# Product of attention, row sums, routing steps and zero rows given other places in the instruction order of a fused attention, MoE and expert kernel

## Chip, cores and metric

One core of a Trainium2 chip. The metric is the device time of one execution in microseconds (us): the median of three timed runs of the kernel before was 1121.9 us (1115.05 to 1123.45).

## What is computed

Three layers in a row on 2304 tokens of width 512. Attention: 32 pairs of batch and head of 576 queries, where of every row of scores only the 32 largest are kept:

```python
scores = scale * np.matmul(q, k.transpose(0, 1, 3, 2))
kth = np.partition(scores, -32, axis=-1)[..., -32:-31]
scores = np.where(scores >= kth, scores, -1e9)
attn = exp(scores - max) / (sum + 1e-9)
x = np.matmul(attn, v)
```

Then a dense layer `softplus(x @ w_in) @ w_out` with 2048 hidden units, and last eight experts: `expert = argmax(x @ w_gate)`, and each token gets `gate * (relu(x @ w1[expert]) @ w2[expert])` from the one expert that it was routed to.

## The kernel before

Five engines run their own instruction streams in order and wait for one another by semaphores. A scheduler at build time sets each stream: blocks of code carry a priority (`tc.high_priority`), and inside `tc.issue_after(x)` the instructions of the block that run on the engine of `x` are put behind `x` in that engine's order. This is an order alone; no semaphore comes with it.

**Part one** is one loop over 72 groups of attention, each of two tiles of 128 rows by 576 scores. Iteration i does the following.

- The scores of group i+1 (`emit_scores`, L372 on TensorE, copied by ScalarE at L380). Their PSUM buffer `ps_s` is a single one, so these matmuls wait until VectorE has read the scores of group i for the last time (L424).
- The search for the 32 largest of group i on VectorE (`emit_softmax`): rows are folded (L408 to L424), then four searches for 8 maxima (L414, L432) with three replacements (L428) between them, so three search rounds j = 0, 1, 2; then the mask (L440, or L443 with L444 on GpSimd). ScalarE takes the exponentials (L421), halves of the result are formed (L448 to L450), and a transposing DMA brings them into `pT` (L452, issued on SyncE's queue SP).
- The product with v of group j = i - 3 (`emit_av`, LAG = 3): matmuls L467 and L469 into the PSUM tile `m`, the row sums that come with it are inverted on VectorE (`rc`, L491 and L493), and ScalarE scales the result with them (L495). In before the product is ordered behind the last matmul of the scores that this very iteration issued, those of group i+1.
- Steps of the dense layer (`some_work`, 1.7 per iteration): units of one or two tiles of tokens, numbered 1 to 10, 16 steps each. A step is `layer1` (12 matmuls L554, softplus on ScalarE, its sum L563 on GpSimd) and, two steps later, `layer2` (L588 with f32 operands, one for each tile; from unit 9 on L585). These are called *dense steps* below.
- After each such step one step of a side queue, which holds generators. `route` (L612 to L663) is one for each finished tile: transposes, gate matmul, VectorE work on the logits, an exponential on ScalarE (L635) whose sum VectorE takes up (`gs`, L636), matmuls for the rank of each token in its expert, and DMAs that write the token's row to `rows` and its place to `table`. In before it is cut by `yield` into five steps. `clear_late` (L664 to L671), queued once unit 1 is done (`ZFILL = 1`), clears an `xr` buffer of the pool `x2p` on GpSimd (L667) and writes 1154 KB of zeros from it with two DMAs (L669) over the rows of tokens that come late. `early_slots` (L673 to L706), queued after unit 7, plans the first five slots of experts: the counts (matmul L676), and then five rounds on VectorE, each giving one pair of values in `early` (L704, L705).

**Part two** runs the slots: SyncE loads the pair of a slot into registers (L824, L825), reads 256 token numbers (`idx`, L829), loads the weights (L833, L836), GpSimd gathers the rows (`xg`, L841), TensorE transposes them (L863) and does the two matrix products (L893, L906). The first slots of part two are scheduled while the last dense steps still run.

The time falls into the attention with dense steps (to 777 us), the last dense steps (777 to 870 us) and the expert slots (870 us to the end).

Of the kernel before, what the change touches and what calls it, by code (L numbers as in the profile page):

```python
# [24 lines left out]
KD = DM // 128  # L25
# [33 lines left out]
C = 512  # L59
LAG = 3  # L60
SCALE = 1
ZFILL = 1
LATE = ((2, 8), (3, 0))
GLAG = 2
XAHEAD = 2
# [104 lines left out]
def part_one(tc, ctx, q, k, v, w_in, w_out, const, ident, before, ones, iota_e, reg_e, wg, ids,  # L170
# [182 lines left out]
        pair[m] = (q1, q2, kt, v16, sc)  # L353

    sc_t, pt_t, o_t, x_t = {}, {}, {}, {}
    tops, last_qk = [None], [None]

    def emit_qk(m, kind, ps, base):
        q1, q2, kt, v16, sc = pair[m]
# [25 lines left out]
    def emit_softmax(gi):  # L385
# [39 lines left out]
        for j in range(3):  # L425
            for i in n:
                to = wk[i] if flags is None else src[i]
                nc.vector.match_replace(out=to, in_to_replace=mx[:, i, 8 * j:8 * j + 8], in_values=src[i],  # L428
                                        imm_value=NEG)
                src[i] = to if flags is None else w2[:, i, :wide[j + 1]]  # L430
            for i in n:
                nc.vector.max(out=mx[:, i, 8 * j + 8:8 * j + 16], in_=src[i])  # L432
        if flags is not None and gi % FLB == FLB - 1:
            g0 = 2 * (gi - FLB + 1)
            nc.vector.tensor_tensor(out=flags[:, g0:g0 + 2 * FLB],
# [105 lines left out]
    def layer1(u):  # L541
# [9 lines left out]
        m = 0  # L551
        for c in range(KD):
            for p, r in ((0, 0), (0, 1), (1, 0)):
                nc.tensor.matmul(hps[:, :n], lhsT=w_in_s[:, c, j, p, o:o + 128], rhs=xT[:, 0:len(u.tiles), r, c, :],  # L554
                                 start=m == 0, stop=m == 3 * KD - 1)
                m += 1
        a = ep.tile([128, 256], F32, name="sa")
        nc.scalar.activation(a[:, :n], hps[:, :n], AF.Abs, scale=down)
# [18 lines left out]
    def layer2(u, f):  # L577
        if f == 0:
            u.y = [ps_y.tile([128, DM], F32, name="y") for _ in u.tiles]
        g = u.g.pop(f)  # L580
        for i in range(len(u.tiles)):
            cs = slice(i * 128, i * 128 + 128)
            if u.number >= TAIL:
                for m, (a, b) in enumerate(PASSES):
                    nc.tensor.matmul(u.y[i], lhsT=g[0][:, a, cs], rhs=g[1][:, b, :], start=f == 0 and m == 0,  # L585
                                     stop=f == KF - 1 and m == 2)
            else:
                nc.tensor.matmul(u.y[i], lhsT=g[:, cs], rhs=w_out_s[:, f, :], start=f == 0, stop=f == KF - 1)  # L588
        if f == KF - 1:
            for i, (key, spans) in enumerate(u.tiles):  # L590
                xr = x2p.tile([128, ROWW], F32, name="xr")
                nc.scalar.activation(xr[:, :DM], u.y[i], AF.Copy, scale=2.0 ** -8)
                side.append(route(xr, spans, ids_col(key), u.number > NU))
            if u.number == ZFILL:
                side.append(clear_late())
            if u.number == NU:
                side.append(early_slots())

# [13 lines left out]
    def route(xr, spans, col, after):  # L612
# [7 lines left out]
        lp = ps_h.tile([128, 512], F32, name="h")  # L620
        for c in range(KD):
            nc.tensor.matmul(lp[:, 0:E], lhsT=x2T[:, c, :], rhs=wg[:, c, :], start=c == 0, stop=c == KD - 1)
        lg = sm.tile([128, E], F32, name="lg")
        nc.vector.tensor_copy(lg, lp[:, 0:E])
        m8 = sm.tile([128, E], F32, name="m8")
# [3 lines left out]
        nm = sm.tile([128, 2], F32, name="nm")  # L629
        nc.vector.tensor_scalar(nm[:, 0:1], m8[:, 0:1], -1.0, None, op0=ALU.mult)  # L630
        nc.vector.tensor_copy(nm[:, 1:2], ix[:, 0:1])
        yield
        ex = sm.tile([128, E], F32, name="ex")
        gs = sm.tile([128, 1], F32, name="gs")
        nc.scalar.activation(ex, lg, AF.Exp, bias=nm[:, 0:1], accum_out=gs)  # L635
        nc.vector.tensor_scalar(gs, gs, 1e-9, None, op0=ALU.add)  # L636
        nc.vector.reciprocal(xr[:, DM:DM + 1], gs)
        oh = sm.tile([128, E], F32, name="oh")
        nc.vector.tensor_scalar(oh, iota_e, nm[:, 1:2], None, op0=ALU.is_equal)
        yield  # L640
        pp = ps_h.tile([128, 512], F32, name="h")
        nc.tensor.matmul(pp[:, 0:E], lhsT=before, rhs=oh, start=True, stop=False)
        nc.tensor.matmul(pp[:, 0:E], lhsT=ones, rhs=ohcum, start=False, stop=True)
        ds = sm.tile([128, E], F32, name="ds")
        nc.vector.tensor_tensor(out=ds, in0=pp[:, 0:E], in1=reg_e, op=ALU.add)
        nc.vector.tensor_tensor(out=ohcum, in0=ohcum, in1=oh, op=ALU.add)
# [17 lines left out]
    def clear_late():  # L664

        z = x2p.tile([128, ROWW], F32, name="xr")
        nc.gpsimd.memset(z, 0.0)  # L667
        for b, r0 in LATE:
            nc.sync.dma_start(rows[b * S:b * S + S, :].rearrange("(p r) a -> p r a", r=R)[:, r0:],  # L669
                              z[0:64].rearrange("p (o a) -> p o a", o=1).to_broadcast([64, R - r0, ROWW]))  # L670
        yield  # L671

    def early_slots():  # L673

# [68 lines left out]
    for i in range(-1, n + LAG):  # L743
# [15 lines left out]
        if to_scale and to_scale[0][1] <= i:  # L759
            with tc.high_priority(offset=AHEAD):  # L760
                prep_scale(to_scale.pop()[0])
        if i == -1:
            decode_some(2)
        if i + 1 < n:
            with tc.high_priority(offset=A_SC):
                emit_scores(i + 1)
        if 0 <= i < n:
            with tc.high_priority(offset=AHEAD):
                emit_softmax(i)
# [1 line left out]
                decode_some(DECR)  # L771
        j = i - LAG
        if j >= 0:
            with tc.high_priority(offset=A_AV), ExitStack() as behind_scores:
                if i + 1 < n:

                    behind_scores.enter_context(tc.issue_after(last_qk[0].ins))
                for x in groups[j]:
                    emit_av(*x)
            for u in units.get(j, []):  # L780
# [273 lines left out]
```

## Time and profile before

| | us |
|---|---|
| median of three timed runs | 1121.9 |
| lowest, highest | 1115.05, 1123.45 |
| the profiled execution | 1126.11 |
| its span in the trace | 1124.4 |

The profile is one execution. Its span is 1.7 us shorter than its time, and its time is 4.2 us above the median of the timed runs. Mean granted TensorE clock: 0.936. In the rows below PE is TensorE's matmuls, PEld its weight loads, DVE is VectorE, ACT ScalarE, POOL GpSimd, SP SyncE; SPq and POOLq are the DMA queues that these two issue on. A number in brackets behind a row is the time that the engine was idle ahead of it, with what ended that. Names without numbers are the program's tiles.

### The profile page before, as it was taken

To read this page: it belongs to the slowest core of one execution; us is meant where nothing else is said; L and a number is where in the kernel's file an instruction comes from. 1 tells how busy PE (TensorE), PEld (TensorE's weight loads), DVE (VectorE), ACT (ScalarE), POOL (GpSimd) and SP (SyncE) were. 2 spreads that over 40 slices of the span, in tenths; PEclk is the share of its full clock that TensorE was granted. 3 is DMA by queue.
4 is the path that set the end of the run, shared out by engine and by line. 5 is a ranking of instruction groups with operands and counts; after the bars stand their busy time and mean duration, and the time that the engine had idled before them with its cause. 6 is when DMAs were issued, how large, how long until landed. Compare 5 with 4: busy or idle time off the path is not lost.

```text
span 1124.4 us, 22653 instructions
## 1 busy us (share of the span) xinstructions
PE 895.9 (80%) x7146; PEld 646.0 (57%) x7146; DVE 948.4 (84%) x2980; ACT 798.7 (71%) x1898; POOL 638.0 (57%) x731
## 2 busy tenths in 40 slices
PE   1133257766887887899989999999999999999992
PEld 0012144433554564666556666566778889999981
DVE  4999999999968787999989899999556887767771
ACT  5767678886657777877888787877689655555560
POOL 3888889887466666766777666757423112111110
PEclk9996578997988898999999999999999999999996
DMA  8897788885467789635766664444601566666550
GB/s 191 193 197 157 175 179 168 182 193 108 71 110 110 135 137 137 126 74 96 145 131 125 104 106 74 83 74 82 201 19 24 119 234 223 250 206 246 201 189 18
DMA packets 295881, 157.18 MB, mean 140 GB/s; under 512 B 257524, under 2 KB 257652, under 8 KB 295732
## 3 DMA queue, kind: packets, MB, share of 16 engines
q1 hardware_dynamic: 292116, 145.73, 60.1%
q0 software_dynamic: 3616, 9.72, 2.5%
q8 instruction: 62, 1.02, 0.4%
q14 instruction: 87, 0.71, 0.3%
HBM read 77.89 MB, written 11.11 MB: 79 GB/s over the span
## 4 chain that ended last, share of the span: by engine, by line
PE 34%; DVE 28%; DMA 13%; issue 8%; POOL 7%; ACT 6%; SPq 2%; POOLq 0%; ACTq 0%; DVEq 0%
PE h L893 8%; PE y L906 8%; DVE mx L432 6%; PE h L554 5%; DVE wk L428 5%; PE y L588 4%; DMA pT<-p 4%; DVE xr L216 3%; DVE mk L443 2%; PE y L585 2%; POOL p L450 2%; DVE e L440 2%; DVE wk L424 2%; DMA w<-in_moe_w_in_dram 1%; POOL g L563 1%
## 5 line engine op out<-in xcount | busy, mean ns | idle before, releaser
L588 PE MATMUL y<-w_out_s,g 128*128 128x512 f32 x480 | 244.2, 634 | 31.3 <-POOL g L563 31.0
L554 PE MATMUL h<-xT,w_in_s 128*128 128x256 f16 (+1 forms) x1920 | 226.6, 268 | 23.4 <-DMA xT<-xh 10.1
L554 PEld LDWEIGHTS <-w_in_s 128*128 128x128 f16 x1920 | 173.6, 101 | 95.3 <-issue 60.3
L372 PE MATMUL s<-kt,q 128*128 128x512 f16 (+7 forms) x640 | 97.8, 315 | 131.5 <-DVE wk L424 87.7
L432 DVE MAX8 mx<-wk 128x8 f32<-128x144 f32 (+2 forms) x432 | 199.6, 494 | 0.2
L563 POOL TENSOR_TENSOR g<-g,sa 128x256 f32<-128x256 f32 (+1 forms) x160 | 118.7, 745 | 101.7 <-ACT sa L562 93.6
L450 POOL TENSOR_TENSOR p<-e,p 128x512 f16<-128x512 f32 x144 | 169.2, 1175 | 0.0
L448 ACT ACTIVATE p<-e 128x576 f16<-128x576 f32 x144 | 98.2, 684 | 73.6 <-DMA pT<-p 35.2
L372 PEld LDWEIGHTS <-q 128*128 128x128 f16 (+1 forms) x640 | 44.6, 107 | 174.9 <-DVE wk L424 70.9
L588 PEld LDWEIGHTS y<-w_out_s,g 128*128 128x128 f32 x480 | 86.5, 201 | 101.8 <-issue 61.3
L428 DVE MATCH_REPLACE8 wk<-mx,wk 128x144 f32<-128x144 f32 (+1 forms) x432 | 144.5, 340 | 0.1
L444 POOL TENSOR_TENSOR e<-e,mk 128x576 f32<-128x576 f32 x84 | 109.6, 1307 | 47.7 <-DVE mk L443 25.9
L873 POOL DMA_INDIRECT out_dram<-ot,idx x19 | 19.9, 1045 | 177.5 <-DVE ot L872 174.8
L893 PEld LDWEIGHTS h<-xT,wf 128*128 128x128 f32 x864 | 111.9, 191 | 5.3 <-ACT wf L854 0.2
L893 PE MATMUL h<-xT,wf 128*128 128x256 f32 x864 | 114.0, 283 | 0.0
L906 PE MATMUL y<-wf,hT 128*128 128x512 f32 x432 | 112.7, 399 | 0.0
L421 ACT ACTIVATE e<-s,bias 128x576 f32<-128x576 f32 x144 | 105.8, 770 | 2.1 <-POOL p L450 0.9
L467 PE MATMUL m<-v,pT 128*128 128x65 f16 (+1 forms) x1440 | 92.3, 200 | 9.7 <-ACT x L495 8.4
L467 PEld LDWEIGHTS <-pT 128*128 128x128 f16 (+1 forms) x1440 | 85.5, 105 | 16.3 <-issue 12.5
L906 PEld LDWEIGHTS y<-wf,hT 128*128 128x128 f32 x432 | 76.8, 189 | 13.2
L380 ACT ACTIVATE s<-s 128x1152 f32<-128x1152 f32 x72 | 80.5, 1119 | 4.8 <-PE s L372 4.7
L469 PE MATMUL m<-v,pT 128*128 128x64 f16 (+1 forms) x800 | 75.7, 200 | 0.0
(193 smaller groups left out, 1900.2 us busy)
## 6 DMA issues: line engine op xcount, KB each, us to landing
w1r<-in_moe_w_dram SPq DMA_DIRECT2D x20, 1024.0 KB, 5.1
w2r<-in_moe_w_dram SPq DMA_DIRECT2D x20, 1024.0 KB, 6.5
w<-in_moe_w_in_dram SPq DMA_DIRECT2D x16, 512.0 KB, 6.5
w<-in_moe_w_out_dram SPq DMA_DIRECT2D x16, 512.0 KB, 4.3
rows<-xr SPq DMA_DIRECT2D x37, 128.2 KB, 2.7
qn<-in_q_dram SPq DMA_DIRECT2D x16, 288.0 KB, 3.3
kn<-in_k_dram SPq DMA_DIRECT2D x16, 288.0 KB, 3.1
vn<-in_v_dram SPq DMA_DIRECT2D x16, 288.0 KB, 3.0
```

The source lines that it names most:

```text
L372: last_qk[0] = nc.tensor.matmul(ps[p0:p1, base + k0 * D:base + k1 * D], lhsT=lhs, rhs=kt[:, k0:k1, cs], start=first, stop=not first)
L421: nc.scalar.activation(e[i], s[i], AF.Exp, bias=bt[:, i], scale=SCORE if flags is not None else sc[i][:, 3:4])
L428: nc.vector.match_replace(out=to, in_to_replace=mx[:, i, 8 * j:8 * j + 8], in_values=src[i], imm_value=NEG)
L432: nc.vector.max(out=mx[:, i, 8 * j + 8:8 * j + 16], in_=src[i])
L444: nc.gpsimd.tensor_tensor(out=e[i], in0=e[i], in1=mk, op=ALU.mult)
L450: nc.gpsimd.tensor_tensor(out=p16[:, S + D:], in0=e[i][:, 0:S - D], in1=p16[:, 0:S - D], op=ALU.subtract)
L467: nc.tensor.matmul(o[:, h, 0:D + 1], lhsT=pT(r), rhs=v16[:, h, c, 0:D + 1], start=r == 0, stop=r == R - 1)
L554: nc.tensor.matmul(hps[:, :n], lhsT=w_in_s[:, c, j, p, o:o + 128], rhs=xT[:, 0:len(u.tiles), r, c, :], start=m == 0, stop=m == 3 * KD - 1)
L563: nc.gpsimd.tensor_tensor(out=g, in0=g, in1=a[:, :n], op=ALU.add)
L588: nc.tensor.matmul(u.y[i], lhsT=g[:, cs], rhs=w_out_s[:, f, :], start=f == 0, stop=f == KF - 1)
L893: nc.tensor.matmul(h, lhsT=w1f[:, a, c, :], rhs=xT[:, b, c, :], start=n == 0, stop=n == 3 * KD - 1)
L906: nc.tensor.matmul(y[i], lhsT=hT[g][:, a, i * 128:i * 128 + 128], rhs=w2f[:, b, :], start=g == 0 and n == 0, stop=g == KF2 - 1 and n == 2)
```

## The change

Four edits in part one.

1. *Product.* The product of group j is no longer ordered behind the scores of group i+1, but behind what had been issued on TensorE when the iteration began: the scores of group i (three groups on from j) and the last matmul of the dense steps. In the order it now stands ahead of the scores of group i+1.
2. *Row sums.* L491 and L493 are ordered behind the last MAX of the second search round (j = 1) of group i.
3. *Routing.* `route` has six steps for five: there are new cuts after the gate matmul, after the exponential and after the rank matmuls, and two older ones go.
4. *Zero rows.* `clear_late` is called at iteration 10, before any unit is done, and no longer from the side queue.

```diff
-ZFILL = 1
+ZFILL = 10
@@ emit_softmax
             for i in n:
-                nc.vector.max(out=mx[:, i, 8 * j + 8:8 * j + 16], in_=src[i])
+                ins = nc.vector.max(out=mx[:, i, 8 * j + 8:8 * j + 16], in_=src[i])
+                if j == 1:
+                    last_round[0] = ins
@@ layer1 (and the same for the f32 matmul of layer2)
-                nc.tensor.matmul(hps[:, :n], lhsT=w_in_s[:, c, j, p, o:o + 128], ...
+                last_moe[0] = nc.tensor.matmul(hps[:, :n], lhsT=w_in_s[:, c, j, p, o:o + 128], ...
@@ layer2
-            if u.number == ZFILL:
-                side.append(clear_late())
@@ route
             nc.tensor.matmul(lp[:, 0:E], lhsT=x2T[:, c, :], rhs=wg[:, c, :], ...
+        yield
...
         nc.vector.tensor_copy(nm[:, 1:2], ix[:, 0:1])
-        yield
...
         nc.scalar.activation(ex, lg, AF.Exp, bias=nm[:, 0:1], accum_out=gs)
+        yield
...
         nc.vector.tensor_scalar(oh, iota_e, nm[:, 1:2], None, op0=ALU.is_equal)
-        yield
...
         nc.tensor.matmul(pp[:, 0:E], lhsT=ones, rhs=ohcum, start=False, stop=True)
+        yield
@@ part one, loop
+        anchors = [x[0] for x in (last_qk, last_moe) if x[0]]
...
                 emit_scores(i + 1)
+        if i == ZFILL:
+            clear_late()
...
-            with tc.high_priority(offset=A_AV), ExitStack() as behind_scores:
-                if i + 1 < n:
-                    behind_scores.enter_context(tc.issue_after(last_qk[0].ins))
+            with tc.high_priority(offset=A_AV), ExitStack() as order:
+                for x in anchors:
+                    order.enter_context(tc.issue_after(x.ins))
+                if i < n:
+                    order.enter_context(tc.issue_after(last_round[0].ins))
                 for x in groups[j]:
                     emit_av(*x)
```

From L435 on the lines of the changed kernel are some two further down (L491 is L493 there, L588 is L590), in part two seven (L829 is L836).

**Place 1, the middle of the attention.** On TensorE in before, around the product into `m_6778`; `s_6591` are the scores of group i and `s_6725` those of group i+1, `h_` tiles are layer 1 and `y_` tiles layer 2 of dense steps:

```order
L372 MATMUL s_6591<-kt_4646,q1_4644 128x512
...
L467 MATMUL m_6648<-v16_5733,pT_6220 128x65
...
L588 MATMUL y_7262<-w_out_s_151,g_7422 128x512
L554 MATMUL h_7582<-xT_6832,w_in_s_150 128x256
...
L554 MATMUL h_7743<-xT_6832,w_in_s_150 128x256
...
L372 MATMUL s_6725<-kt_4952,q1_4950 128x512
...
L467 MATMUL m_6778<-v16_5733,pT_6376 128x65
```

The same place on TensorE in the changed kernel:

```order
L372 MATMUL s_6581<-kt_4639,q1_4637 128x512
...
L643 MATMUL h_7458<-oh_7456,before_66 128x8
L556 MATMUL h_7550<-xT_6832,w_in_s_150 128x256
...
L590 MATMUL y_7262<-w_out_s_151,g_7413 128x512
L556 MATMUL h_7579<-xT_6832,w_in_s_150 128x256
...
L469 MATMUL m_6778<-v16_5733,pT_6362 128x65
...
L372 MATMUL s_6725<-kt_4938,q1_4936 128x512
```

The product into `m_6778` has moved from behind the scores `s_6725` to ahead of them, behind the dense steps of the iteration before.

On VectorE in before, at the row sums `rc_6807` of that product:

```order
L428 MATCH_REPLACE wk_6739<-mx_6457,wk_6739 128x288 x2
L432 MAX mx_6457<-wk_6739 128x8 x2
L440 SCALAR_TENSOR_TENSOR e_6735<-s_6590,mx_6457,e_6735 128x576
L443 TENSOR_SCALAR mk_6763<-s_6590,mx_6457 128x576
L491 TENSOR_SCALAR rc_6807<-m_6778 128x2
L408 TENSOR_TENSOR s_6725<-s_6725,s_6724 128x288
L493 RECIPROCAL rc_6807<-rc_6807 128x2
```

The same row sums on VectorE in the changed kernel:

```order
L428 MATCH_REPLACE wk_6739<-mx_6441,wk_6739 128x144 x2
L432 MAX mx_6441<-wk_6739 128x8 x2
L493 TENSOR_SCALAR rc_6807<-m_6778 128x2
L428 MATCH_REPLACE wk_6739<-mx_6441,wk_6739 128x288 x2
L495 RECIPROCAL rc_6807<-rc_6807 128x2
L432 MAX mx_6441<-wk_6739 128x8 x2
L408 TENSOR_TENSOR s_6725<-s_6725,s_6724 128x288
```

The row sums have moved from the end of the search of group i to the point behind its second round, one replacement and one MAX earlier.

**Place 2, the end of the attention.** On TensorE in before, from the counts of `early_slots` (`h_11139`) to the first transposes of the first slot (`tp_12653`); between them lie ten layer 1 steps, of which the first and the last stand here:

```order
L676 MATMUL h_11139<-ohcum_80,ones_67 128x8
L554 MATMUL h_11143<-xT_10732,w_in_s_150 128x256
...
L467 MATMUL m_10509<-v16_7618,pT_10130 128x65
...
L467 MATMUL m_10656<-v16_8350,pT_10401 128x65
...
L554 MATMUL h_11458<-xT_11194,w_in_s_150 128x256
...
L863 MATMUL tp_12653<-ident_61,xg0_12613 128x128 x2
```

The same stretch on TensorE in the changed kernel:

```order
L677 MATMUL h_11192<-ohcum_80,ones_67 128x8
L469 MATMUL m_10653<-v16_8350,pT_10394 128x65
...
L556 MATMUL h_11196<-xT_10732,w_in_s_150 128x256
...
L556 MATMUL h_11227<-xT_10732,w_in_s_150 128x256
...
L556 MATMUL h_11255<-xT_11181,w_in_s_150 128x256
...
L556 MATMUL h_11290<-xT_11181,w_in_s_150 128x256
...
L870 MATMUL tp_12653<-ident_61,xg0_12613 128x128 x3
```

Between the counts and the first transposes four layer 1 steps are left of ten, and one product of three.

On SyncE in before, the loads of pairs of `early` ahead of the first `idx`:

```order
L452 DMA_TRANSPOSE pT_10407<-p16_10403 128x9x128
L516 DMA_TRANSPOSE xT_11194<-xh_11199 128x8x128
...
L824 TENSOR_LOAD early_100
...
L825 TENSOR_LOAD early_100
...
L829 DMA idx_12602<-table_82 128x1
```

On SyncE in the changed kernel:

```order
L454 DMA_TRANSPOSE pT_10400<-p16_10396 128x9x128
L831 TENSOR_LOAD early_100
L831 ISA x2
L832 TENSOR_LOAD early_100
L832 ISA x2
L836 REGISTER_ALU
L836 DMA idx_12602<-table_82 128x1
```

In before the pairs of all five slots are loaded ahead of the first `idx` (ten such loads), in the changed kernel the first slot's pair alone.

**Place 3, the zero rows on GpSimd.** In before, around the MEMSET of `clear_late`:

```order
L563 TENSOR_TENSOR g_3329<-g_3329,sa_3327 128x256
L656 DMA table_82<-ids_90,dsti_3344 18688x1
L667 MEMSET xr_3902 128x513
L563 TENSOR_TENSOR g_3361<-g_3361,sa_3359 128x256
L444 TENSOR_TENSOR e_3502<-e_3502,mk_3529 128x576
```

In the changed kernel:

```order
L217 TENSOR_TENSOR w_out_s_151<-xr_1216,w_1214 128x512
L451 TENSOR_TENSOR p16_2636<-e_2600,p16_2636 128x64
L452 TENSOR_TENSOR p16_2636<-e_2600,p16_2636 128x512
L669 MEMSET xr_1460 128x513
L345 MEMSET vs_3053 128x9x2
L565 TENSOR_TENSOR g_2581<-g_2581,sa_2579 128x256
```

The MEMSET has moved from behind the first routed tile's `table` write to behind the last piece of the weights' decoding (L217).

## Rows read from the trace of the kernel before

**Rows 1.** By stretch: bounds, length, busy PE, PEld, DVE, ACT, POOL; clock; DMA.

```profile
200.00:300.00 100.00, 72.12 (x615) 45.06 (x615) 99.22 (x314) 82.22 (x191) 81.10 (x89) 0.91 0.69 142
300.00:400.00 100.00, 80.38 (x639) 50.51 (x638) 80.76 (x282) 66.06 (x159) 58.13 (x70) 0.90 0.66 117
...
500.00:600.00 100.00, 92.08 (x779) 59.44 (x777) 95.20 (x323) 82.75 (x208) 72.42 (x86) 0.98 0.65 120
600.00:700.00 100.00, 94.52 (x832) 63.11 (x830) 94.86 (x364) 78.71 (x195) 69.68 (x87) 1.00 0.61 100
...
777.00:870.00 93.00, 90.39 (x738) 69.34 (x738) 56.00 (x224) 72.55 (x226) 38.54 (x52) 1.00 0.31 81
870.00:1124.40 254.40, 230.18 (x1462) 206.06 (x1460) 174.63 (x386) 134.08 (x271) 39.42 (x39) 0.97 0.56 187
```

**Rows 2.** VectorE's waits from 300 to 777 us: total us, times, longest.

```profile
DVE rc L491 <- PE m L467: 11.2, 6, 5.5
DVE gs L636 <- ACT ex L635: 7.9, 5, 2.7
...
DVE s L408 <- ACT s L380: 6.8, 11, 1.6
```

**Rows 3.** Timeline 295 to 330 us: start, length, engine, line; idle before and releaser.

```profile
300.19 0.58 SPq L653 DMA_DIRECT2D rows<-xr  x1
...
310.37 0.52 POOL L667 MEMSET xr<- 128x513 f32 x1 [9.62 <-DMA rows<-xr]
...
311.63 3.78 PE L588 MATMUL y<-w_out_s,g 128*128 128x512 f32 x4 [7.06 <-POOL g L563]
...
315.30 0.87 DVE L440 SCALAR_TENSOR_TENSOR e<-s,mx,e 128x576 f32<-128x576 f32 x1 [4.22 <-ACT e L421]
```

**Rows 4.** Timeline of VectorE, 318 to 326 us and 374 to 377 us.

```profile
318.90 0.16 DVE L491 TENSOR_SCALAR rc<-m 128x2 f32<-128x2 f32 x1 [1.83 <-PE m L467]
...
325.55 0.15 DVE L636 TENSOR_SCALAR gs<-gs 128x1 f32<-128x1 f32 x1 [2.71 <-ACT ex L635]
...
375.81 0.16 DVE L491 TENSOR_SCALAR rc<-m 128x2 f32<-128x2 f32 x1 [5.48 <-PE m L467]
```

**Rows 5.** Timeline of TensorE, 366 to 377 us.

```profile
368.51 5.18 PE L554 MATMUL h<-xT,w_in_s 128*128 128x256 f16 x24 [5.00 <-DMA xT<-xh]
```

**Rows 6.** DMA issues: operation, count, KB, median us from issue to landing.

```profile
rows<-xr SPq DMA_DIRECT2D x1, 1154.2 KB, 8.4
...
xg<-rows,idx POOLq DMA_INDIRECT x19, 6.0
```

**Rows 7.** The transposing DMA L452: issue to landing, all 144.

```profile
DMA to landing us min/median/max: 3.2/3.4/10.2
```

**Rows 8.** Timeline of SyncE 594 to 598 us, then of ScalarE 606 to 609 us.

```profile
595.37 2.72 SPq L452 DMA_TRANSPOSE pT<-p  x2
...
607.06 1.12 ACT L380 ACTIVATE s<-s 128x1152 f32<-128x1152 f32 x1
```

**Rows 9.** TensorE by line, 400 to 777 us: count, busy, mean ns, idle before.

```profile
L588 PE MATMUL y<-w_out_s,g 128*128 128x512 f32 x310 | 153.0, 615 | 10.7 <-POOL g L563 10.5
L554 PE MATMUL h<-xT,w_in_s 128*128 128x256 f16 (+1 forms) x1021 | 118.9, 266 | 6.3 <-ACT g L560 5.0 <-DMA xT<-xh 0.8 <-ACT p L448 0.4
```

**Rows 10.** One line's instructions: count, ns min/median/max, first and last start.

```profile
L676 PE MATMUL h<-ohcum,ones x2: 253/254/256, 776.7 to 776.8; 128*128 128x8 f32 x2
L705 DVE CAST early<-ev x5: 142/145/154, 784.2 to 791.9; 128x1 int32<-128x1 f32 x5
```

**Rows 11.** Timeline, 778 to 810 us, of VectorE, SyncE, GpSimd and TensorE.

```profile
778.84 0.15 DVE L678 TENSOR_SCALAR eci<-h 128x8 int32<-128x8 f32 x1
...
793.62 0.93 SPq L829 DMA_DIRECT2D idx<-table  x2
...
797.84 1.01 POOL L841 DMA_INDIRECT xg<-rows,idx  x1 [0.16 <-issue]
...
809.14 0.38 PE L863 MATMUL tp<-ident,xg 128*128 128x128 f32 x2
```

More of the change, by code (lines that the diff above doesn't have):

```diff
@@ L355, in part_one @@
     sc_t, pt_t, o_t, x_t = {}, {}, {}, {}
-    tops, last_qk = [None], [None]
+    tops, last_qk, last_moe, last_round = [None], [None], [None], [None]
     def emit_qk(m, kind, ps, base):
@@ L553, in layer1 @@
             for p, r in ((0, 0), (0, 1), (1, 0)):
-                nc.tensor.matmul(hps[:, :n], lhsT=w_in_s[:, c, j, p, o:o + 128], rhs=xT[:, 0:len(u.tiles), r, c, :],
-                                 start=m == 0, stop=m == 3 * KD - 1)
+                last_moe[0] = nc.tensor.matmul(hps[:, :n], lhsT=w_in_s[:, c, j, p, o:o + 128],
+                                               rhs=xT[:, 0:len(u.tiles), r, c, :], start=m == 0, stop=m == 3 * KD - 1)
                 m += 1
@@ L587, in layer2 @@
             else:
-                nc.tensor.matmul(u.y[i], lhsT=g[:, cs], rhs=w_out_s[:, f, :], start=f == 0, stop=f == KF - 1)
+                last_moe[0] = nc.tensor.matmul(u.y[i], lhsT=g[:, cs], rhs=w_out_s[:, f, :], start=f == 0,
+                                               stop=f == KF - 1)
         if f == KF - 1:
@@ L670, in clear_late @@
                               z[0:64].rearrange("p (o a) -> p o a", o=1).to_broadcast([64, R - r0, ROWW]))
-        yield
     def early_slots():
```

## The prediction

> **What bounds the kernel now.** I read the table by stretch first [rows 1]. Its columns behind the bounds and the length are busy times of TensorE, its weight loads, VectorE, ScalarE and GpSimd. The reader should see three stages. From 200 to 300 us VectorE is busy 99.2 of 100. From 500 to 700 us it still has some 95 of 100, but TensorE has come up to 92 and 94.5: two engines in order, both nearly full. Between them, from 300 to 400, VectorE idles 19.2 and TensorE 19.6, so there the two wait for each other. After 777 us only TensorE counts: it is busy 90.4 of 93 and 230.2 of 254.4, VectorE 56 of 93. So what the change saves in the attention must come out of VectorE's idle time, and what it adds to TensorE after 777 is paid almost in full.
>
> Next I read what VectorE waits for between 300 and 777 us [rows 2]: row sums that wait for the product 11.2 us, the routing sum `gs` that waits for ScalarE's exponential 7.9, the fold that waits for the copied scores 6.8. Then I looked up the longest of these in the timeline. At 310.37 the MEMSET of the zero rows had waited 9.62 us for a row write that had been issued at 300.19, since `xr` was still in use; the dense step's sum L563 is queued behind it on GpSimd, the f32 matmul of layer 2 came 7.06 late, and VectorE's L440 4.22 [rows 3]. In the same knot VectorE waited 1.83 at the row sums and 2.71 at `gs` [rows 4]. At the start of unit 2 layer 1 waited 5.00 for its transposed input [rows 5]; the product queued behind it on TensorE made the row sums wait 5.48 [rows 4].
>
> **The change part by part.** It adds no arithmetic: the same matmuls, searches, DMAs. All of it is order, so each term is a wait that goes or comes. The sum is made against the profiled execution's 1126.1 us (span 1124.4 plus 1.7 around it) and carried over to the median, 4.2 us lower.
>
> *Zero rows.* At the old place 4.22 + 1.83 + 2.71 = 8.8 us of VectorE's idle time hang on the MEMSET [rows 3, 4]. At the new place the MEMSET follows the last decoding on GpSimd, whose use of the buffer GpSimd itself ends, so it waits for no DMA (place 3 of the order). What is queued behind it: on GpSimd 0.52 us of MEMSET; on SyncE's queue a load of v and transposes of two tiles, behind 1154 KB whose writing took 8.4 us at the old place [rows 6]. There VectorE idles only 0.8 of 100 [rows 1], so a late transfer that reached it would show in full: 0 to 8.4. The products that need these transposes stand three groups later, some 30 us, so I take 1.5. Term: -8.8 + 1.5 = **-7.3** (bounds -8.8 and -0.4).
>
> *Product and row sums.* The row sums wait 11.2 us, of which 1.83 is already counted: 9.4 [rows 2, 4]. In the changed order the product is issued ahead of the scores of the next group, which have to wait for VectorE's last read, and the row sums come a search round earlier on VectorE. So the product leads by the wait of these scores and the row sums give back less than a round. The new wait is that the product, now ahead of the scores, holds them up when the transposed `pT` is late. Queued behind are those scores, ScalarE's copy, and VectorE's fold L408. Group 51 shows the margin: its transposes are issued at 595.37 and land 3.4 later in the median [rows 7, 8], at 598.8; the scores three groups on are copied at 607.06 [rows 8], so the product is ready some 8 us ahead, and even the slowest landing of 10.2 us [rows 7] would end at 605.6. At unit starts [rows 5] the wait is TensorE's own and stays. I take two thirds of 9.4: **-6.2** (bounds -9.4, and +4 if two of 144 landings are so late that the scores lose 2 us each).
>
> *Routing.* `gs` waits 7.9, less the 2.71 counted: 5.2 [rows 2, 4]. With the exponential and its sum in separate steps, ScalarE has one dense step more to come to it. But ScalarE's stream has other work ahead of it. I take half: **-2.6** (bounds -5.2 and 0). Six steps for five put the last units' rank later by a dense step for each tile; that is no work, it moves `early_slots`, and is in the tail below.
>
> Attention together: -7.3 - 6.2 - 2.6 = **-16.1**, and at most 8.8 + 9.4 + 5.2 = 23.4. It is gained in full only if VectorE sets the pace; TensorE at 92 to 94.5 is close behind [rows 1], and what is late next is its layer 2, waiting for L563 (10.7 us from 400 to 777 [rows 9]), and the fold.
>
> *Dense steps left over.* A layer 1 is 12 matmuls, some 1.45 us in a row; a layer 2 of two tiles shows as four rows and takes 1.8 (from busy times of 118.9 and 153.0 us for 1021 and 310 rows that overlap [rows 9], 1.40 and 1.97). Counted in both orders, when the last scores are issued, the changed kernel has done one layer 1 and one layer 2 less and two transposes of routing (0.55). So TensorE has 1.45 + 1.8 + 0.55 = **+3.8** more after the attention.
>
> *Wait for the first gather.* In before ten layer 1 steps stand between the counts at 776.7 [rows 10] and the first transposes at 809.14 [rows 11]: 32.4 us of cover. In the changed order four layer 1, three layer 2 and one product are left (place 2): 4 x 1.45 + 3 x 1.8 + 0.85 = 12.05, by the rows' stretch (32.4 measured where the same costs give 31.2) 12.5. Against it the chain: counts to `eci` 0.6 when VectorE is free (2.1 in before, at 778.84 [rows 10, 11]); `eci` to the first pair 784.2 - 778.84 = 5.4; pair to `idx` 793.62 - 791.9 = 1.7, as only the first pair is loaded ahead of it now (in before the fifth, 7.7 us later); `idx` to the gather 797.84 - 793.62 = 4.2; the gather 6.0 [rows 6, 10, 11]. Sum 17.9, so TensorE stands still for 17.9 - 12.5 = **+5.4**. Bounds: 0, and 797.84 + 6.0 - 776.7 - 12.5 = 14.6 if the chain takes as long as before.
>
> By the Trainium skill ("DMA: Bandwidth & Descriptors", on the SWDGE path) a GpSimd DMA costs about 2.0 us plus its bytes over 436 GB/s; for 128 rows of 2 KB that is an estimated 2.6 us, and the wait would be 2.0. The rows of this kernel show 6.0, and the sum goes by them.
>
> Net: -16.1 + 3.8 + 5.4 = **-6.9**; 1126.1 - 6.9 = 1119.2 for an execution like the profiled one, 1121.9 - 6.9 = **1115.0** for the median. About 1% (11 us) is what a measurement of this kernel can tell from no change, so this lies within it.
>
> **Rivals.** *A, faster: the tail gives its two terms back.* If TensorE has slack after 777, or the pair and the gather come early, 3.8 and 5.4 go: 1121.9 - 16.1 = 1105.8, and with all waits gone 1121.9 - 23.4 = 1098.5. For it: the steps of before are covered with room, VectorE idles 40% there. Against it: TensorE idles 2.6 of 93 from 777 to 870 [rows 1]. The Trainium skill ("Perfetto Trace Analysis", Identifying the Most-Contended Engine) would side with it: TensorE is to be judged by weight loads, not by busy matmuls, and these are 69.3 of 93. The matmul rows lie end to end there, so the trace speaks against it.
>
> *B, slower: the gather takes as long as before.* If VectorE's rounds of `early_slots` are again spread between other work, the wait is 14.6. With 3.8 left over and only the zero rows gained (-7.3), that is +11.1: 1133.0. It decides from a wait above 16.1 - 3.8 = 12.3 on, against all gains. For it: VectorE's plan took 15.2 us from counts to the fifth pair [rows 10]. Against it: SyncE now asks for the first pair alone.
>
> *C, no gain: the waits move.* VectorE's waits for the row sums come back as waits of the fold for the scores (6.8 now [rows 2]), since the product holds the scores or TensorE is the pace. Then -7.3 for the zero rows stands against 3.8 + 5.4: 1121.9 + 1.9 = 1123.8.
>
> **How the numbers follow.** Forecast 0.38, its own range 1108 to 1122; A 0.32; B 0.18; C 0.12. Faster by over 1% (below 1110.7): all but little of A and a quarter of the forecast, 0.32 + 0.10 = 0.42. Slower by over 1% (above 1133.1): half of B and a quarter of C, 0.14 with 0.02 for a landing that stalls more. Within 1%: 0.44. The range takes in A to its end at 1098.5, rounded down, and B's 1133 and a little above: 1097 to 1134.
>
> **What would show it.** Right: from 300 to 400 us VectorE is busy over 85; its waits at the row sums between 300 and 777 are below 5 us; the MEMSET waits for nothing long; dense steps end some 10 us earlier by the clock, and TensorE idles about 5 us ahead of the first transposes of L870, released by the gather. Wrong: the fold L408 waits over 12 us; TensorE waits over 12 us for the gather; or TensorE's idle time in the tail stays at 2.6 and the whole gain arrives.

## The result, and the profile after

The changed kernel took 1131.2 us (median of seven runs, 1127.71 to 1133.87) against 1121.9: the ratio is 1.010 with a 95% interval of 1.0074 to 1.0126. It is slower by 1%, where a gain of 0.6% was forecast. The profiled execution took 1131.93 us, its span 1130.2, 5.8 more than in before.

The table by stretch of the changed kernel (columns as in [rows 1]):

```profile
300.00:400.00 100.00, 84.61 (x756) 55.69 (x753) 89.39 (x324) 75.27 (x184) 67.41 (x80) 0.92 0.70 118
500.00:600.00 100.00, 91.50 (x767) 59.33 (x766) 94.46 (x329) 82.96 (x203) 72.97 (x88) 0.96 0.79 135
600.00:700.00 100.00, 92.17 (x796) 61.30 (x794) 94.42 (x351) 77.34 (x190) 64.80 (x80) 0.98 0.58 87
777.00:870.00 93.00, 85.60 (x630) 65.59 (x629) 47.98 (x198) 65.22 (x203) 29.26 (x41) 0.96 0.21 66
```

VectorE's busy time from 300 to 400 us rose from 80.8 to 89.4, as forecast. But TensorE's fell by 4.8 us between 777 and 870. By the clock of the traces the last scores end at 753.0 us (762.6 in before), a gain of 9.6, and the last dense step's matmul at 879.7 (875.6), a loss of 4.1: the stretch between them, called the tail below, grew from 113.0 to 126.7. What follows it is 1.7 us longer.

VectorE's waits from 300 to 777 us in the changed kernel, for [rows 2]:

```profile
DVE s L408 <- ACT s L380: 14.6, 8, 4.9
DVE rc L493 <- PE m L469: 13.7, 8, 6.1
...
DVE gs L638 <- ACT ex L636: 0.9, 2, 0.7
```

`gs` fell from 7.9 to 0.9. The row sums did not fall (11.2 before) and the fold went from 6.8 to 14.6. One of the fold's waits, on ScalarE and VectorE:

```profile
607.88 0.68 ACT L343 ACTIVATE vs<-vn 128x576 f16<-128x576 f32 x1 [5.10 <-DMA v<-vs]
608.47 1.11 ACT L380 ACTIVATE s<-s 128x1152 f32<-128x1152 f32 x1
...
609.62 0.47 DVE L408 TENSOR_TENSOR s<-s 128x288 f32<-128x288 f32 x1 [4.93 <-ACT s L380]
```

ScalarE stood 5.10 us in front of a split of v, since the buffer `vs` was still being read by DMAs; the copy of the scores is queued behind it, and the fold behind that. What was late is a DMA of line L348 to L350, issued about 599 to 600 us. GpSimd's and SyncE's timelines there:

```profile
598.17 1.01 POOL L658 DMA_INDIRECT table<-ids,dsti  x1 [0.15 <-issue]
...
598.95 0.60 SPq L348 DMA_DIRECT2D v<-vs  x1
599.59 0.62 SPq L349 DMA_DIRECT2D v<-vs  x1
```

They were issued right behind the indirect DMA that writes a tile's places into `table`. By the landing records that table write landed at 605.7, the load of 598.95 at 606.05. Not every DMA has such a record; of line L348 it is 5 of 32 loads in the changed kernel, and over these five:

```profile
DMA to landing us min/median/max: 2.3/3.1/9.0
```

In before the same line has 2.3/2.3/4.3, over 15 of its 32 loads.

The zero rows went as forecast; the MEMSET waits for nothing:

```profile
252.34 0.52 POOL L669 MEMSET xr<- 128x513 f32 x1
```

In the tail TensorE waits for the first gather, and then for something that was not forecast (timelines of TensorE, SyncE, GpSimd and ScalarE):

```profile
795.01 0.44 PE L870 MATMUL tp<-ident,xg 128*128 128x128 f32 x2 [2.47 <-DMA xg<-rows,idx]
...
852.85 2.58 SPq L655 DMA_DIRECT2D rows<-xr  x2
...
854.84 1.20 POOL L658 DMA_INDIRECT table<-ids,dsti  x1 [0.66 <-DVE dsti L652]
...
860.64 0.60 ACT L595 ACTIVATE xr<-y 128x512 f32<-128x512 f32 x1 [5.14 <-DMA rows<-xr]
...
862.20 0.52 PE L587 MATMUL y<-w,vn 128*128 128x512 f32 x1 [4.82 <-ACT vn L576]
```

A row write issued at 852.85, with a table write beside it, landed only at 860.5; ScalarE's copy into the same buffer `xr` waited 5.14 us, and TensorE 4.82. After that idle stretch its granted clock was at the lower level, 1.2 GHz, for 8 us and more:

```profile
864.00:872.00 8.00, 8.00 (x42) 6.59 (x42) 2.96 (x14) 4.27 (x19) 0.92 (x2) 0.50 0.07 17
872.00:876.00 4.00, 4.00 (x37) 3.38 (x37) 2.09 (x9) 3.51 (x15) 1.90 (x3) 0.90 0.17 41
```

At 0.50 of the clock 8 us hold 4 us of work at the full clock, so an estimated 4 us were lost there. By these estimates the tail adds up: one dense step and one routing more left over 4.9 us, gather 2.5, the wait 4.8, the slow clock some 4.5, less a wait of 2.4 us for a product at 784 us of before that is gone: 14.3, where 13.7 was measured.

### The profile page after: what moved, and what is told of

Its sections match the earlier page's. It is cut to its first block, busy times and chain, and to the rows that moved or that the text cites. A ratio compares the mean times of both kernels' runs of the same rounds, so it can differ in the third digit from the quotient of the medians.

```text
span 1130.2 us, 22634 instructions
## 1 busy us (share of the span) xinstructions
PE 900.6 (80%) x7146; PEld 650.3 (58%) x7146; DVE 948.8 (84%) x2980; ACT 802.0 (71%) x1898; POOL 637.7 (56%) x731
## 4 chain that ended last, share of the span: by engine, by line
PE 36%; DVE 26%; DMA 14%; issue 8%; POOL 7%; ACT 6%; SPq 3%; POOLq 0%; ACTq 0%; DVEq 0%
PE h L900 9%; PE y L913 9%; DVE mx L432 5%; PE h L556 5%; DVE wk L428 5%; DMA pT<-p 5%; PE y L590 4%; PE y L587 3%; DVE mk L445 3%; POOL p L452 2%; DMA q<-st 2%; DMA v<-vs 2%; DVE wk L424 2%; DVE e L442 2%; DVE xr L216 2%
## 5 line engine op out<-in xcount | busy, mean ns | idle before, releaser
L590 PE MATMUL y<-w_out_s,g 128*128 128x512 f32 x480 | 238.4, 621 | 24.3 <-POOL g L565 24.3
L372 PE MATMUL s<-kt,q 128*128 128x512 f16 (+7 forms) x640 | 104.4, 328 | 102.4 <-DVE wk L424 67.1
L565 POOL TENSOR_TENSOR g<-g,sa 128x256 f32<-128x256 f32 (+1 forms) x160 | 116.1, 729 | 104.3 <-ACT sa L564 93.4
L452 POOL TENSOR_TENSOR p<-e,p 128x512 f16<-128x512 f32 x144 | 167.1, 1160 | 0.0
L446 POOL TENSOR_TENSOR e<-e,mk 128x576 f32<-128x576 f32 x84 | 112.0, 1336 | 60.7 <-DVE mk L445 35.8
L590 PEld LDWEIGHTS y<-w_out_s,g 128*128 128x128 f32 x480 | 85.1, 197 | 93.3 <-issue 61.5
L450 ACT ACTIVATE p<-e 128x576 f16<-128x576 f32 x144 | 98.1, 682 | 55.3 <-POOL e L446 14.6
L469 PEld LDWEIGHTS <-pT 128*128 128x128 f16 (+1 forms) x1440 | 85.4, 105 | 41.0 <-issue 39.4
L471 PEld LDWEIGHTS <-pT 128*128 128x128 f16 (+1 forms) x800 | 60.8, 105 | 32.8 <-issue 32.5
```

The lines of the kernel that those rows point to most:

```text
L372: last_qk[0] = nc.tensor.matmul(ps[p0:p1, base + k0 * D:base + k1 * D], lhsT=lhs, rhs=kt[:, k0:k1, cs], start=first, stop=not first)
L446: nc.gpsimd.tensor_tensor(out=e[i], in0=e[i], in1=mk, op=ALU.mult)
L452: nc.gpsimd.tensor_tensor(out=p16[:, S + D:], in0=e[i][:, 0:S - D], in1=p16[:, 0:S - D], op=ALU.subtract)
L469: nc.tensor.matmul(o[:, h, 0:D + 1], lhsT=pT(r), rhs=v16[:, h, c, 0:D + 1], start=r == 0, stop=r == R - 1)
L565: nc.gpsimd.tensor_tensor(out=g, in0=g, in1=a[:, :n], op=ALU.add)
L590: last_moe[0] = nc.tensor.matmul(u.y[i], lhsT=g[:, cs], rhs=w_out_s[:, f, :], start=f == 0, stop=f == KF - 1)
```

## Experiments

Each ratio is to runs of the kernel before on the same chip, with its 95% interval. Several chips were used, on which the kernel before had medians from 1119.2 to 1122.5 us; across experiments the ratios compare better than the microseconds.

### The parts of the change

Routing in five steps again, the rest of the change kept (three of the moved cuts):

```diff
             nc.tensor.matmul(lp[:, 0:E], lhsT=x2T[:, c, :], rhs=wg[:, c, :], start=c == 0, stop=c == KD - 1)
-        yield
...
         nc.vector.tensor_copy(nm[:, 1:2], ix[:, 0:1])
+        yield
...
         nc.scalar.activation(ex, lg, AF.Exp, bias=nm[:, 0:1], accum_out=gs)
-        yield
```

> The changed kernel with routing in five steps as before; product, row sums and zero rows stay changed. Theory 1 (six steps keep the row buffer xr one dense step longer, so near 855 us ScalarE's copy into xr waits 5.14 us for the row write, TensorE stands still 4.82 us and then runs at a granted clock of 0.50 from 864 to 872 us): that wait and the half clock go, some 9 us, less the 7 us that VectorE's gs waits gave back in the attention, of which half is worth time: about 1131.2 - 9 + 3.5 = 1125.5, with no ScalarE wait above 1 us at xr<-y after 845 us. Rival 2 (the product's order costs the time: one dense step more left over, 4.9 us, and 13.7 us of row sum waits): the time stays at 1131 or rises by the gs waits to 1134.

Measured 1125.1 us, ratio 1.0028 (1.0006 to 1.0051). The sixth step costs 6 us. The wait at `xr<-y` is gone, `gs` waits 10.9 us again.

Six steps, but the row writes in the fifth:

```diff
-        yield
         for p0, n, t0, st in spans:
             wr = nc.sync.dma_start(rows[t0:t0 + (n - 1) * st + 1:st, :], xr[p0:p0 + n, :])
             if after:
                 late.append(wr)
+        yield
```

> The changed kernel, all six routing steps kept, but the row writes stand in the fifth step, one dense step earlier; the table write stays in the sixth. Theory 1: the wait of 5.14 us at xr<-y and the half clock behind it go while the gs waits stay low (0.9 us): 1131.2 - 9 = about 1122. Rival 2 (product's order): no change, 1131.

Measured 1117.3 us (its runs lie far apart, from 1106.3 to 1123.4), ratio 0.9915 (0.9875 to 0.9955): 14 us less, more than was expected, and faster than before. But the reason given for it failed: the copy into `xr` still waited,

```profile
850.28 0.60 ACT L595 ACTIVATE xr<-y 128x512 f32<-128x512 f32 x1 [4.86 <-DMA rows<-xr]
```

and 5.5 of the 11.4 us by which this span is shorter are gained before the last scores.

The order of product and row sums alone, put into the kernel before:

```diff
 # before.py
+        anchors = [x[0] for x in (last_qk, last_moe) if x[0]]
...
-                    behind_scores.enter_context(tc.issue_after(last_qk[0].ins))
+                for x in anchors:
+                    order.enter_context(tc.issue_after(x.ins))
+                if i < n:
+                    order.enter_context(tc.issue_after(last_round[0].ins))
```

> The kernel before with the new order of product and row sums alone; zero rows and five routing steps as before. Theory 1: the order is not what costs, 1118 to 1124 (attention a few us shorter, one dense step more left over, gather wait of about 2.5 us). Rival 2: slower than before by 5 us and more, 1127 or above.

Measured 1133.4 us, ratio 1.009 (1.0056 to 1.0124). Rival 2's number, so the order costs too. The longest wait stands on VectorE, behind one of ScalarE:

```profile
316.49 1.25 ACT L450 ACTIVATE p<-e 128x576 f16<-128x576 f32 x2 [9.45 <-DMA pT<-p]
...
320.52 0.47 DVE L408 TENSOR_TENSOR s<-s 128x288 f32<-128x288 f32 x1 [9.68 <-ACT s L380]
```

A transposing DMA was late. Two transfers were under way beside it: the zero rows, which this kernel still writes at the old place (issued at 300.94 and 301.44, landed at 309.7), and a table write issued at 304.42. The two transposes that SyncE issued from 302.14 on landed at 316.5 and 316.7. The same kernel without table writes (`b_order_notable`, below) parts the two: there the zero rows are issued at 300.10 and 300.60, the two transposes from 301.30 on land at 310.1 and 311.3, ScalarE's wait is 3.34 + 0.59 us and VectorE's 3.57. By this comparison some 3.5 of the 9.7 us belong to the zero rows and 6 to the table write.

Zero rows early alone:

```diff
 # before.py
-ZFILL = 1
+ZFILL = 10
...
+        if i == ZFILL:
+            clear_late()
```

> The kernel before with the zero rows early alone. My term of the prediction: -7.3 us (bounds -8.8 to -0.4), so about 1114.6, with the MEMSET waiting for no DMA and the 7.06 us wait of layer 2 near 311 us gone. Rival: what is gained near 311 us is taken back before the end of the attention by the next wait, 1120 to 1122.

Measured 1121.6 us, ratio 0.9997 (0.9975 to 1.002): nothing, so the rival holds. Beside the new order the same edit is worth 8 us (`b_order` 1133.4, with early zero rows `a_five` 1125.1). These parts do not add.

### How early the row writes must be, and the order by itself

Row writes in the fourth step, behind the rank matmuls:

> The changed kernel, six routing steps, the row writes now in the fourth step (two dense steps earlier than the change has them). In the kernel with them in the fifth the copy into xr still waited 4.86 us at 850 us for a row write. Theory 1 (the row buffer xr held too long by six steps is the price): this wait goes below 1 us, TensorE's idle time of 3.9 us and the half clock behind it too, so some 6 us less than with the fifth step: about 1111. Rival (the row writes helped in the attention alone, the wait in the tail is not worth anything): 1117.

Measured 1111.4 us, ratio 0.9924 (0.9900 to 0.9948): the fastest of the complete kernels in us, equal by its ratio to the fifth step's. The copy's wait is down to 1.77 us.

The order undone in the kernel with row writes in the fifth step:

> The kernel before with zero rows early, six routing steps and the row writes in the fifth, but the product and the row sums ordered as before. Against the changed kernel with row writes in the fifth step (1117.3) it undoes the order alone. If the order of product and row sums costs time in any setting (it cost 10.9 us alone and about 3.5 beside early zero rows): 1107 to 1114. If it pays once the routing waits are gone: 1120 and above.

Measured 1124.1 us, ratio 1.0031 (1.0003 to 1.0060). By the ratios the order pays 1.2% here, where alone it cost 0.9%.

The order split in two, each half alone in the kernel before; first the product, then the row sums:

> The kernel before with the product alone ordered as in the change; row sums free, zero rows and five routing steps as before. Theory: the 10.9 us of the order come from the product ahead of the next scores (its wait passes to the fold L408, whose waits rise from 7.6 to 22.8 us after 200 us): 1130 to 1134. Rival: they come from the row sums behind the second search round: 1122.

> The kernel before with the row sums alone behind the second search round; product, zero rows and routing as before. Theory (product is what costs): within 3 us of 1122.5. Rival (VectorE stands at the row sums in the middle of the search because the product, behind the scores, is not there yet): 1130 and above, with row sum waits over 20 us.

Measured 1123.9 us (1.0038, 1.0016 to 1.0060) and 1127.8 us (1.0077, 1.0053 to 1.0102). Neither expectation holds: each half costs something, and neither shows the waits that were named (row sums wait 4.0 us after 200 us in the second, where over 20 were expected). The halves together, 0.4% and 0.8%, do not differ from the 0.9% of the whole by more than the intervals allow; but neither has the cause that was named for it.

### The side queue in the tail

```diff
-            if side:
-                next(side[0], None)
+            for _ in range(2 if len(side) > 2 else 1):
...
```

> The changed kernel with its late row writes, but the side queue is served twice per dense step while more than two generators stand in it (that is only after early_slots has come in). In the instruction order the second copy into xr of unit 9 then stands behind 146 layer 1 steps, where it stands behind 154 in the changed kernel and 150 in before. Theory 1 (the side queue is too long for the tail: 6 and 17 steps of routing and planning, then 12, against 16 dense steps of a unit): the 5.14 us wait at xr<-y near 860 us, the TensorE wait of 4.82 us behind it and the half clock go, and the time falls by 9 us or more to 1122 or below, without a row write moved. Rival (the late row writes cost by their place in SyncE's queue or in the attention, not by the side queue's length): 1128 to 1131.

> Row writes in the fourth step and the side queue served twice as well. Theory 1: both shorten the same hold, of which 1.77 us of ScalarE's wait are left with the fourth step alone, so little more: 1108 to 1112, and this is the fastest or equal to the fastest version.

Measured 1127.0 us (1.0071, 1.0046 to 1.0096) and 1117.5 us (0.9969, 0.9942 to 0.9997). The waits of `xr<-y` for a row write go in both. The first is 4 us better than the change, though the two intervals overlap, and its tail is 122.1 us long for 126.7: so much, some 4 us, the hold of `xr` can be worth. Together with early row writes the edit loses 6 us. So the hold explains some 4 of 20 us, and the expectation of 9 was wrong.

### Where the row writes cost

```diff
+        if not after:
+            write_rows()
         yield
...
+        if after:
+            write_rows()
```

> The changed kernel (1131.2) with row writes in the fourth step for units 1 to 7 alone, whose routing ends inside the attention; units 8 to 10 keep theirs in the sixth. All units in the fourth step gave 1111.4, 19.8 less. Theory 1 (the hold of xr in the tail): this part keeps the tail stall, and gives at most the 8 us that serving the side queue twice left unexplained: 1123 to 1131. Theory 3 (the late row writes cost in the attention, since they then leave together with the table write and slow the loads of v and the transposes beside them: landings of v up to 9.0 us against 4.3 before, fold waits of 4.9 us at 610): 1115 to 1121.

> The counterpart: row writes in the fourth step for units 8 to 10 alone. Theory 1: most of the 19.8 us, 1113 to 1120, no ScalarE wait over 2 us at xr<-y after 840 us. Theory 3: only the 4 us that the side queue served twice gave: 1125 to 1128.

Measured 1115.3 us (0.9951, 0.9926 to 0.9977) for units 1 to 7 and 1127.0 us (1.0048, 1.0014 to 1.0082) for units 8 to 10: 15.9 and 4.2 us less than the change, together about the 19.8 of all units. So the row writes of units 1 to 7 carry most of it. That does not put it into the attention: of the 16.6 us by which the span of `a_r4_first7` is shorter, 7.5 are gained before the last scores (745.5 us for 753.0), and its tail is 115.2 us for 126.7. The copy's wait in the tail is down to 1.2 us there, although units 8 to 10 write as late as in the change; with their writes alone moved it stays at 4.7. The hold by six steps alone can't be the reason for that wait.

### Without table writes

Here I counted landings over the traces of the nine complete kernels that have records of them, from the end of a DMA's issue, for DMAs from 200 us on. Where a table write was under way (issued less than 2 us later or still in flight; 8 us are taken where its own landing is not recorded), `pT` landed after 4.0 us in the median (79 DMAs, longest 10.3) and else after 2.0 (267, longest 4.1); v after 3.9 against 1.7, row writes after 3.8 against 1.9. The next five kernels leave out the 18 table writes, so tokens get no place in an expert's list and the experts work on the empty row.

```diff
-        wr = nc.gpsimd.indirect_dma_start(out=table, out_offset=bass.IndirectOffsetOnAxis(ap=dsti[:, :1], axis=0),
-                                          in_=ids[:, col:col + 1], in_offset=None)
...
```

> The changed kernel without the 18 table writes of routing (left out: tokens get no place, so the experts work on the empty row). In 14 traces DMAs issued while a table write is under way land later: pT 4.0 us behind the end of its issue against 2.0, v 4.0 against 1.7, row writes 5.8 against 1.9. Theory 3 (late row writes cost because they and what follows them on SyncE fall into the table write's flight): the last scores end at about 745 us as with early row writes (753.0 in the changed kernel), the wait at xr<-y near 860 us falls below 2 us, and the time to that of the next kernel within 4 us. Rival (the hold of xr, or SyncE's order, costs without any table write): the last scores stay at 750 to 755 us and the gap of the two kernels stays 12 us or more.

> Row writes in the fourth step and no table writes (left out as in the kernel ahead). Theory 3: 1105 to 1112, the same as the kernel ahead within 4 us. Rival: faster than it by 12 us and more, as with the table writes (1111.4 against 1131.2).

Measured 1093.8 and 1094.4 us, both 0.9751 (0.9711 to 0.9791). The 19.8 us between the two places of the row write are gone, as Theory 3 had it, but both kernels are faster than it expected; the last scores of the first end at 729.2 us, where 745 were expected. The expert slots are not what got shorter: from the last dense to the last expert matmul it is 217.2 us in the first of them, 218.5 in the change. Then before, the order alone, and the change with five steps:

> The kernel before without the 18 table writes (left out: tokens get no place). It gives the time from which the change is to be counted when no table write is under way. Theory 3 (the change itself pays about what was forecast, and table writes that now fall beside more urgent DMAs take it back): 1100 to 1108, so that the changed kernel without table writes (1093.8) is 6 to 14 us faster than it. Rival (the change is a loss in itself): 1093 or less.

> The kernel before with the new order of product and row sums alone, without table writes (left out). With table writes the order cost 10.9 us. Theory 3: without them it costs nothing or pays, within 3 us of the kernel ahead or faster. Rival (the scores held by the product cost by themselves): 8 to 12 us slower than the kernel ahead.

> The changed kernel with routing in five steps and without table writes (left out). With table writes the sixth step cost 6.1 us. Theory 3: without them six steps are no loss: 1093 to 1100 here against 1093.8 with six. Rival (the sixth step costs by itself): 1088.

They measured 1095.8, 1096.8 and 1094.9 us (0.9787, 0.9757 to 0.9817; 0.9791, 0.9749 to 0.9833; 0.9773, 0.9741 to 0.9805). Without table writes five kernels that lie between 1111.4 and 1133.4 us with them lie within 3 us of one another. Theory 3's numbers were met for the second and the third; for before neither theory's were. The change is no loss in itself, and no gain of 6 to 14 us either; against before it is 2 us, and the intervals overlap.

It is not the row writes at that place that make the transposes late: in the four of these kernels that still write rows in the last step, none of the 62 recorded `pT` issued from 2 us before to 8 us behind a row write landed later than 3.7 us by this count (median 2.0). In the same four kernels with table writes, 18 of 56 took over 5 us.

VectorE's waits in the kernel before without table writes, 300 to 777 us:

```profile
DVE rc L491 <- PE m L467: 5.7, 3, 2.9
DVE s L408 <- ACT s L380: 3.8, 4, 1.2
DVE e L440 <- ACT e L421: 2.4, 2, 1.4
...
DVE gs L636 <- ACT ex L635: 1.2, 1, 1.2
```

Row sums 5.7 for 11.2, `gs` 1.2 for 7.9, with no order changed [rows 2].

## Why the prediction was wrong

**The step that failed** is the one that priced each wait by its own place in the order, -16.1 us for the attention, with the flights of the table writes at nothing. In the profiled executions the attention gave 9.6 us, and the tail took 13.7 where 3.8 + 5.4 = 9.2 were forecast. Without table writes the order is left by itself: the last scores of the change then end 3.1 us earlier than those of before (729.2 against 732.3 us), and its tail is 4.0 longer (115.6 against 111.6). Before itself gains 30.3 us up to its last scores when the table writes go, with no order changed.

**What bounds.** The two readings stood: VectorE and TensorE share the attention, TensorE alone has the tail. What was missed is why they wait in the attention. The chain of waits of before held it, in late transposes, and GpSimd's timeline names the time:

```profile
478.18 7.85 DMA pT<-p
...
678.11 9.61 DMA pT<-p
```

```profile
478.30 1.00 POOL L656 DMA_INDIRECT table<-ids,dsti  x1
...
678.16 1.00 POOL L656 DMA_INDIRECT table<-ids,dsti  x1 [0.15 <-issue]
```

Each of the two lies at a table write. So do all five transposes of before that took over 7 us to land (7.9 to 10.2): they were issued within 2.6 us of one. So does the knot that I read most from: the row write issued at 300.19 kept the MEMSET 9.62 us [rows 3], and a table write had been issued at 299.60. ([rows 7] is not over all 144 transposes but over the 76 that have a landing record.)

**Zero rows, -7.3.** The MEMSET's wait went, as argued. The time did not: alone the edit gave nothing. What failed is putting 8.8 us down to the MEMSET's place. In before without table writes the MEMSET still stands at the old place, at 300.65 us, behind a row write issued at 297.88, and it waits for no DMA: the 9.62 us were the table write's. Which wait takes the gain back when the MEMSET alone is moved is open: the profiled execution of `b_zearly` is the fastest of its twelve (1114.2 us) and can't tell.

**Product and row sums, -6.2.** Wrong in sign: the order alone cost 10.9 us. The row sums' waits did not fall in the profile of the change (13.7 us, 11.2 before), though 4.7 of them come behind the last scores, where VectorE has little else to do. The fold's waits grew by 7.8 us, and the sign to watch for came, but not by the mechanism that was named: the product did not hold the scores. At each of the seven waits of the fold above 0.3 us the scores had been ready 1.9 to 7.2 us before ScalarE's copy, and ScalarE came to the copy from other work without a pause. Three waits, of the fold (3.5 and 4.9) and of the row sums (6.1), make 14.5 of VectorE's 28.3 us; in each ScalarE had stood 5.1 to 7.0 us shortly before at a buffer that DMAs were still reading, and a table write had been issued 10 to 12 us before that ended. The longest, on ScalarE in the changed kernel, with the table write issued at 386.54:

```profile
398.36 0.68 ACT L330 ACTIVATE st<-kn 128x576 f16<-128x576 f32 x1 [7.01 <-DMA q<-st]
```

I priced the new wait from one group in which nothing was late [rows 7, 8]. The longest landing of 10.2 us stood in those rows, and I gave it room for two cases of 144, where five of 76 took over 7 us.

**Routing, -2.6, and "six steps are no work".** `gs` gave back 7.0, more than forecast. But the sixth step moved the row and table writes against everything else on the DMA queues. Undone it is worth 6 us, and with the row writes earlier 14 to 20: the place of these writes alone decides between 1% slower and 0.8% faster than before, and it had no term.

**Left over, +3.8: 4.9** by estimate (the routing's gate matmuls were forgotten). **Gather, +5.4: 2.5**, the mechanism as forecast, the chain 14.0 us (781.0 to 795.0) for 17.9. The tail's further 9 us, the wait at `xr` and the slow clock, had no term.

**Rivals.** B's figure of 1133 is near by luck, its mechanism did not come: the gather cost 2.5, not 14.6. That 1131 lies inside the stated range is owed to B's end of it, so to luck as well. C's sign is right in the attention (waits moved to the fold), though not its cause. A did not come.

Shown is that table writes carry the differences among these kernels, and that DMAs issued beside them land late. The traces also show that it need not be bytes that are waited for. In three of the waits above, the knot of before, the late transposes of `b_order` and the late row write in the tail of the change, no DMA moved data for 3.5 to 6 us on end while the landing was awaited (last two columns, the DMA engines' busy share and GB/s; one line for each):

```profile
304.00:310.00 6.00, 0.57 (x5) 0.33 (x3) 5.97 (x24) 1.83 (x6) 0.00 (x0) 0.88 0.00 0
312.00:317.00 5.00, 1.33 (x4) 0.36 (x3) 0.00 (x0) 0.51 (x1) 0.00 (x0) 0.92 0.00 0
857.00:861.00 4.00, 0.38 (x4) 0.14 (x2) 0.00 (x0) 0.36 (x1) 0.00 (x0) 1.00 0.00 0
```

In the trace a DMA leaves sixteen completion marks, and it has landed with the last. Those of the table write in `b_order` come from 313.05 to 316.26, and each mark of the transpose issued at 302.14 follows one of them by 0.15 to 0.20 us; without table writes (`b_order_notable`) the sixteen of this transpose lie within 0.15 us. Open is what makes the marks wait for one another; the two DMAs were issued on different queues, and no run separated a DMA engine from the memory behind it. Open too is which DMAs of each order fell into a flight and cost its time; and a kernel without table writes also has 18 us less work on GpSimd.

## What to carry to other kernels

When waits of several kinds are spread over an engine, look for one transfer that is under way at all of them before each is priced by its own place: here an indirect write of 512 bytes, 18 times, was behind more than half of them: VectorE's waits for row sums, `gs` and fold fell from 25.9 to 10.7 us without it. Edits that only reorder then moved the time by anything from -20 to +11 us, and what an edit was worth depended on the others. Take the suspected transfer out of both kernels first; if the difference goes, move or merge that transfer, and don't tune the order. The best complete kernel here is the change with its row writes in the fourth routing step, ratio 0.9924.

## What the runs showed of the hardware

- The indirect write of 128 words to `table` took 7.5/8.2/11.1 us from issue to landing in the changed kernel (12 of its 18 have a record), longer than the gather of 128 rows of 2 KB (6.2 in the median of the same trace):

```profile
DMA to landing us min/median/max: 7.5/8.2/11.1
```

- While it is under way, other DMAs take about twice as long to land (4.0 against 2.0 us for `pT`), and for up to 6 us of that no DMA moves data (share 0.00 from 304 to 310 us in before); the whole kernel without these writes took 1093.8 us for 1131.2.
- A 4.8 us stop of TensorE was followed by 8 us at a granted clock of 0.50.
